# The first expert's start: two chunks of weights ahead of the gathers, another order of remainders, one comparison a round, rounded digits

## Chip, cores, metric

The kernel runs on one core of a Trainium2 chip. The metric is the device time of one execution in microseconds, as the median of several runs.

## What is computed

An attention with a causal window of 64 positions (8 batches, 8 heads, 576 positions, 64 channels) gives x, 4608 tokens of 512. A mixture of eight experts follows. Every (token, expert) pair is taken in falling order of its logit; a token goes to the first expert that still has room (576 places each). Each expert then runs its tokens through two products.

```python
logits = x @ w_gate
order = np.argsort(-logits.flatten())
for idx in order:
    tok, e = (int(idx) // E, int(idx) % E)
    if assigned[tok] >= 0 or counts[e] >= cap:
        continue
    assigned[tok] = e
    counts[e] += 1
for e in range(E):
    mask = assigned == e
    h = np.maximum(x[mask] @ w1[e], 0.0)
    out[mask] = h @ w2[e]
```

## The kernel before

Three phases lie behind one another on one core. The attention runs for about 148 us and stores x to xs in HBM. Then a routing finds, expert by expert, the threshold at which the fullest expert is filled. `Routing.steps(p)` does this for the p-th expert to be filled: for p = 0 in six rounds (`rounds`, L514) with nothing else for TensorE to do, for p = 1 to 6 in eight rounds (L657 to L780) beside the products of the expert before, for p = 7 none.

A round compares the maxima m (36 columns of 128 tokens) with 15 thresholds (`compare`, L497, in two halves of 20 and 16 columns) into G, and TensorE counts by matmuls over G (L672). When the threshold is known, the places of the taken tokens are numbered. Y (L824) holds each token's place, si its place counted from zero, sb its two digits (place div 32 and place mod 32). A (L849) marks the high digit among 18 values, B (L839) the low digit among 32. R (L851 on ScalarE, L857 on VectorE) is A times the row of the token in two parts, and 18 matmuls of R and B (L862) put the tokens' rows at their places; ils (L866), eight small matmuls (L871) and idx (L876) turn that into the list of 576 row numbers. After it, eid, un and L are brought up to date (L881 to L889) and the choices counted (L892, L896); `taken` (L899) adds the count up with one matmul (L901) and three small operations.

`Experts.turn` (L1110) gathers the rows of the list by five indirect DMAs on GpSimd's queue (L1132; four tiles of 128 rows and one of 64), transposes each tile (`across`, L1051), copies it to xh (L1122, ScalarE, rounded) and makes the remainder xl = x - xh (L1126, VectorE). `Experts.load` (L966) fetches the weights in eight chunks of 512 KB (four of w1, four of w2) into st, copies each to hi (L1017, ScalarE) and makes the remainder lo, either on VectorE (L1021, for p = 0 in the chunks 0 to 2) or by a copy on ScalarE (L1026) and an accumulating DMA on GpSimd's queue (L1028). For p = 0 the chunks 0 to 3 are fetched by SyncE's queue before the list is ready, the others by GpSimd's.

`Experts.steps` (L1271) runs the first product in units of 128 hidden columns f by 256 or 320 tokens: twelve matmuls each into one of three PSUM rooms (`room`, L957), four of hi with xh, four of lo with xh, four of hi with xl. `evac` copies the room to hh (L1280, ScalarE) and makes hl (L1285, VectorE). Two units share a chunk of w1. For p = 0 six units of the first 256 tokens come first, then six of the other 320, then the last two f. `warm` (L603) puts matmuls that feed nothing into TensorE's queue: 28 behind the list of p = 0 and six behind the first tile's transposes.

Every engine works its queue off in order. The order is fixed while the program is written: generators (`route`, `load`, `turn`, `products`) yield either an estimated time or a condition, and `Streams.run` (L1415) resumes them by a clock of its own, so that what an instruction stands behind in its queue depends on the estimates. For p = 0 `turn` puts the transposes of tile a at the moment there - 1.28 us x (4 - a), where there is 9.3 us behind the writing of the list (6.4 for the gathers, 2.9 for their landing).

Of the kernel before, what the change touches and what calls it, by code (L numbers as in the profile page):

```python
# [9 lines left out]
FT = mybir.dt.float32  # L10
# [353 lines left out]
FAR = 2.0 ** 101  # L364
OWN = 2
# [5 lines left out]
class Routing:  # L371


    def __init__(self, ctx, tc, c, V):
        self.tc, self.nc, self.c, self.V = tc, tc.nc, c, V
        nc = tc.nc
        rt = ctx.enter_context(tc.tile_pool(name="rt", bufs=1))
        self.rt, self.ctx = rt, ctx

        def t(name, shape, dt=FT):  # L380
            x = rt.tile(shape, dt, name=name)
            setattr(self, name, x)
            return x

        for name in ("eid", "un", "m", "best"):
            t(name, [128, NJ])
        for name in ("oh", "w", "one"):
            t(name, [128, NJ, E], BF)
        t("G0", [128, NJ * 64], BF)
        t("hi", [128, NJ], BF)  # L390
        t("cw", [128, E])
        t("dg", [128, 64], I32)
        t("sh", [128, NR], I32)
        t("v5", [72, 2, 4, 5], I32)
        t("lane", [128, 1])
        t("rows", [128, 1], U32)
        self.setup = self.constants(t)
        self.idx, self.eint = {}, {}

# [10 lines left out]
    def constants(self, t):  # L410
# [37 lines left out]
        for name, n, m in (("r32", 32, 2), ("r18", 18, NJ)):  # L448
            yield nc.gpsimd.iota(t(name, [128, n, m], BF), pattern=[[1, n], [0, m]], base=0, channel_multiplier=0,
                                 allow_small_or_imprecise_dtypes=True)  # L450
# [174 lines left out]
    def steps(self, p):  # L625
# [8 lines left out]
        if p < E - 1:  # L634
            if p:
                for n, f in enumerate(self.choices(0, NJ, p)):
                    f()
                    yield self.dve(490)
                    if n == 3 and p > 1:
                        yield from self.taken()  # L640

# [15 lines left out]
            for r in range(NR if p else 0):  # L657
# [4 lines left out]
                for j0, j1 in ((0, 20), (20, 36)):  # L662
                    self.compare(G, thr, j0, j1)
                    yield self.dve(420)
# [161 lines left out]
        si = tile_([128, 3, NJ], I32, name="si", bufs=1)  # L826
        nc.vector.scalar_tensor_tensor(si[:, 0], Y[:, 0], -1.0, Y[:, 1], op0=OP.add, op1=OP.add)
        yield self.dve(500)
        nc.vector.tensor_scalar(si[:, 1], si[:, 0], 5, None, op0=OP.arith_shift_right)
        nc.vector.tensor_scalar(si[:, 2], si[:, 0], 31, None, op0=OP.bitwise_and)  # L830
        sb = tile_([128, 2, NJ], BF, name="sb", bufs=1)
        nc.vector.tensor_copy(sb, si[:, 1:3])
        yield self.dve(500)
# [10 lines left out]
        Rw = R_[:, :, 0:72].rearrange("p q (k a h) -> p k a q h", k=2, h=2)  # L844

        def pairs(x):
            return x.rearrange("p a (q h) -> p a q h", h=2)

        nc.vector.tensor_tensor(A_, self.r18, sb[:, 0, None, :].to_broadcast([128, 18, NJ]), OP.is_equal)  # L849
        yield self.dve(410)  # L850
# [4 lines left out]
        for j0, j1 in ((0, NJ),) if p else ((0, 18), (18, 36)):  # L855
            n = j1 - j0
            nc.vector.tensor_tensor(Rw[:, 1, :, j0 // 2:j1 // 2], pairs(A_[:, :, j0:j1]), pairs(self.row[:, :, j0:j1].to_broadcast([128, 18, n])), OP.mult)  # L857
            if not p:
                low(j0 // 2, j1 // 2)
            yield self.dve(600) + slack + (500 if p else 0) + late  # L860
            for j in range(j0, j1, 2):
                nc.tensor.matmul(il, R_[:, j // 2], B_[:, j // 2].rearrange("p b h -> p (b h)"), start=(j == 0), stop=(j == NJ - 2))  # L862
            yield self.busy(n * 16)
# [8 lines left out]
        if p == 0:  # L872
            self.warm(28)
# [5 lines left out]
        if p < E - 1:  # L879
# [30 lines left out]
            if not p or p == E - 2:  # L910
                yield slack if p < OWN else 1500
                yield from taken()
# [22 lines left out]
class Experts:  # L935
# [30 lines left out]
    def load(self, p, ei):  # L966
# [7 lines left out]
        def fetch(i):  # L974
            st[i] = fw.tile([128, 1024], FT, name="st", bufs=STAGE)

            q, r = (nc.gpsimd, eg) if p == 0 and i >= 4 else (nc.sync, e)
# [8 lines left out]
        for i in range(ahead):  # L986
            fetch(i)
        if p == 0:
            yield lambda: self.gathered

# [12 lines left out]
        jobs = [(i, k) for i in range(2 * NCH) for k in range(2 if seven and i < NCH else 1)]  # L1003
        for i, k in jobs:
# [14 lines left out]
            yield lambda: self.gathered > p  # L1019
# [90 lines left out]
    def turn(self, p, idx):  # L1110
# [19 lines left out]
        for a in range(5):  # L1130
            n = 128 if a < 4 else 64
            nc.gpsimd.indirect_dma_start(out=g[0:n, a], out_offset=None, in_=self.xs,  # L1132
                                         in_offset=IndirectOffsetOnAxis(ap=idx[0:n, a:a + 1], axis=0))
        self.gathered += 1
# [12 lines left out]
        for tiles in ((0, 1), (2, 3), (4,)) if p else ((0,), (1,), (2,), (3,), (4,)):  # L1147
# [6 lines left out]
            if p == 0 and a < 1:  # L1154
                self.warm(6)
# [115 lines left out]
    def steps(self, p, idx):  # L1271
# [29 lines left out]
        for n, (f, c0, c1) in enumerate(units):  # L1301
            yield lambda: (p, f // 2, 0) in self.W
            yield lambda: self.tiles[p] * 128 >= c1
            wh, wl = self.W[p, f // 2, 0]
            h = self.room()[:, 0:c1 - c0]
            k = 0
            for wt, xt in ((wh, xh), (wl, xh), (wh, xl)):
# [3 lines left out]
                for cc in range(NX):  # L1311
                    nc.tensor.matmul(h, wv[:, cc, 128 * (f % 2):128 * (f % 2) + 128], xt[:, cc, c0:c1],  # L1312
                                     start=(k == 0), stop=(k == 11))
                    k += 1
                    if k % 3 == 0:
                        yield self.busy(3 * (13.5 + (c1 - c0) / 2.4))
            self.spawn(evac(f, c0, h), 100)
# [115 lines left out]
def body(tc, q, k, v, vt, wg, w1, w2, xs, out):  # L1433
    nc = tc.nc
    with ExitStack() as ctx:
# [13 lines left out]
        rt.spare = ex.room  # L1449
# [43 lines left out]
```

## Time and profile before

| | us |
|---|---|
| median of 3 runs | 643.43 |
| the runs | 643.63, 640.76, 643.43 |
| the profiled execution | 638.62 |
| its span, first to last instruction | 636.4 |
| TensorE (PE) busy | 603.9 (95%) |
| VectorE (DVE) busy | 461.6 (73%) |
| ScalarE (ACT) busy | 339.5 (53%) |
| GpSimd (POOL) busy | 217.4 (34%) |

The profile is of one execution, and its times are microseconds from its first instruction. Some 2.2 us lie outside the span. Names such as L1021 are lines of the kernel before. "out<-in" gives the tiles that an instruction writes and reads; a bracket gives the idle time of the engine just before the instruction and what ended it. PEld is the loading of weights into TensorE, SP is SyncE.

### The profile page before, as it was taken

To read this page: it belongs to the slowest core of one execution; us is meant where nothing else is said; L and a number is where in the kernel's file an instruction comes from. 1 tells how busy PE (TensorE), PEld (TensorE's weight loads), DVE (VectorE), ACT (ScalarE), POOL (GpSimd) and SP (SyncE) were. 2 spreads that over 40 slices of the span, in tenths; PEclk is the share of its full clock that TensorE was granted. 3 is DMA by queue.
4 is the path that set the end of the run, shared out by engine and by line. 5 is a ranking of instruction groups with operands and counts; after the bars stand their busy time and mean duration, and the time that the engine had idled before them with its cause. 6 is when DMAs were issued, how large, how long until landed. Compare 5 with 4: busy or idle time off the path is not lost. (4 is left out here: it accounts for less than half of the span.)

```text
span 636.4 us, 16942 instructions
## 1 busy us (share of the span) xinstructions
PE 603.9 (95%) x6395; PEld 525.3 (83%) x6395; DVE 461.6 (73%) x2043; ACT 339.5 (53%) x596; POOL 217.4 (34%) x231
## 2 busy tenths in 40 slices
PE   7899999995589999999999999999999999999995
PEld 6778888885479779988998898899789889988984
DVE  5888878887787757876786787678768776885610
ACT  2477767681255176345637446363626556666820
POOL 4355556551141061224306123331522422323211
PEclk9999999996599999999999999999999999999999
DMA  8997769993477098769679677948948556856821
GB/s 316 370 377 290 293 251 346 357 360 127 149 222 136 23 305 203 149 226 205 165 172 264 178 151 265 228 104 230 234 150 191 179 145 164 258 138 157 183 62 41
DMA packets 39760, 133.04 MB, mean 209 GB/s; under 512 B 5112, under 2 KB 5240, under 8 KB 39680
## 3 DMA queue, kind: packets, MB, share of 16 engines
q0 software_dynamic: 14992, 51.93, 36.0%
q1 hardware_dynamic: 24400, 79.52, 34.7%
q8 instruction: 50, 0.82, 0.5%
q10 hardware_dynamic: 288, 0.52, 0.3%
q14 instruction: 30, 0.25, 0.1%
HBM read 82.15 MB, written 18.87 MB: 159 GB/s over the span
## 5 line engine op out<-in xcount | busy, mean ns | idle before, releaser
L1341 POOL DMA_INDIRECT out<-ot,idx x40 | 40.6, 1016 | 196.3 <-ACT ot L1326 33.7
L1359 PE MATMUL o<-wh,hh 128*128 128x512 f32 x256 | 101.6, 397 | 0.0
L1359 PE MATMUL o<-wl,hh 128*128 128x512 f32 x256 | 101.6, 397 | 0.0
L1359 PE MATMUL o<-wh,hl 128*128 128x512 f32 x256 | 101.4, 396 | 0.0
L152 POOL TENSOR_TENSOR st<-st,mx 128x512 f32<-128x512 f32 x72 | 73.3, 1039 | 67.7 <-DVE mx L145 54.2
L1017 ACT ACTIVATE wh<-st 128x1024 fp32r<-128x1024 f32 x72 | 75.3, 1052 | 16.0 <-DVE st L999 9.0
L1280 ACT ACTIVATE hh<-h 128x256 fp32r<-128x256 f32 (+1 forms) x96 | 38.9, 407 | 71.2 <-PE h L1312 69.4
L1028 POOL DMA_DIRECT2D wl<-st x59 | 54.6, 1143 | 57.2 <-ACT wl L1026 33.0
L1132 POOL DMA_INDIRECT xg<-xs,idx x40 | 43.0, 1075 | 83.1 <-DVE eq L883 72.9
L1312 PE MATMUL h<-xh,wh 128*128 128x320 f32 (+1 forms) x384 | 70.4, 301 | 0.7 <-ACT xh L1122 0.7
L1312 PE MATMUL h<-xh,wl 128*128 128x320 f32 (+1 forms) x384 | 71.0, 300 | 0.0
L145 DVE CUSTOM_DVE_ANT_0 st<-Sp,mask 128x128 f32<-128x128 f32 x288 | 67.7, 284 | 3.1 <-PE Sp L136 2.5
L1312 PE MATMUL h<-xl,wh 128*128 128x320 f32 (+1 forms) x384 | 69.2, 298 | 0.7 <-DVE xl L1126 0.7
L1026 ACT ACTIVATE wl<-wh 128x1024 fp32r<-128x1024 f32 x59 | 62.3, 1056 | 0.8
L1312 PEld LDWEIGHTS h<-xh,wh 128*128 128x128 f32 x384 | 57.0, 189 | 1.5 <-ACT xh L1122 0.8
L1312 PEld LDWEIGHTS h<-xl,wh 128*128 128x128 f32 x384 | 56.9, 189 | 0.9 <-DVE xl L1126 0.9
L1312 PEld LDWEIGHTS h<-xh,wl 128*128 128x128 f32 x384 | 57.1, 189 | 0.2
L1359 PEld LDWEIGHTS o<-wh,hh 128*128 128x128 f32 x256 | 48.1, 188 | 9.6 <-DVE t L1213 0.6
L1359 PEld LDWEIGHTS o<-wh,hl 128*128 128x128 f32 x256 | 48.1, 188 | 9.3
L1359 PEld LDWEIGHTS o<-wl,hh 128*128 128x128 f32 x256 | 48.1, 188 | 9.0
L1326 ACT ACTIVATE ot<-o 128x512 f32<-128x512 f32 x34 | 20.2, 595 | 65.3 <-PE o L1359 61.9
L1285 DVE SCALAR_TENSOR_TENSOR hl<-h,hh 128x256 fp32r<-128x256 f32 x96 | 40.1, 418 | 14.3 <-ACT hh L1280 14.0
(276 smaller groups left out, 1256.8 us busy)
## 6 DMA issues: line engine op xcount, KB each, us to landing
st<-w SPq DMA_DIRECT2D x60, 512.0 KB, 6.6
wl<-st POOLq DMA_DIRECT2D x59, 512.0 KB, 7.0
V<-v SPq DMA_DIRECT2D x16, 584.0 KB, 8.9
xs<-x SPq DMA_DIRECT2D x36, 256.0 KB, 4.3
VT<-vt SPq DMA_DIRECT2D x8, 640.0 KB, 9.0
VT<-vt SPq DMA_DIRECT2D x8, 512.0 KB, 7.7
Q<-q SPq DMA_DIRECT2D x6, 640.0 KB, 7.0
K<-k SPq DMA_DIRECT2D x6, 640.0 KB, 8.4
```

The lines of the kernel that those rows point to most:

```text
L145: nc.vector.tensor_tensor_reduce(st[:, h, :], Sp[h % 2][:, h // 2], mk, scale=-0.125, scalar=3.0e38, op0=OP.add, op1=OP.min, accum_out=mx[ ...
L152: nc.gpsimd.tensor_tensor(st, st, mx[:, :, None].to_broadcast([128, 4, 128]), OP.subtract)
L1017: nc.scalar.activation(hi, x, AF.Copy)
L1026: nc.scalar.activation(lo, hi.bitcast(FT), AF.Copy, scale=-1.0)
L1028: nc.gpsimd.dma_start(lo.bitcast(FT), x, accum_op=OP.add)
L1132: nc.gpsimd.indirect_dma_start(out=g[0:n, a], out_offset=None, in_=self.xs, in_offset=IndirectOffsetOnAxis(ap=idx[0:n, a:a + 1], axis=0))
L1280: nc.scalar.activation(hh[:, f, c0:c1], h, AF.Relu)
L1285: nc.vector.scalar_tensor_tensor(t, h[:, a - c0:b - c0], 0.0, hh[:, f, a:b].bitcast(FT), op0=OP.max, op1=OP.subtract)
L1312: nc.tensor.matmul(h, wv[:, cc, 128 * (f % 2):128 * (f % 2) + 128], xt[:, cc, c0:c1], start=(k == 0), stop=(k == 11))
L1326: nc.scalar.activation(ot, o, AF.Copy)
L1341: nc.gpsimd.indirect_dma_start(out=self.out, out_offset=IndirectOffsetOnAxis(ap=idx[0:m, a:a + 1], axis=0), in_=ot[0:m], in_offset=None)
L1359: nc.tensor.matmul(o, ht[:, f, 128 * a:128 * a + 128], wt[:, 512 * (f % 2):512 * (f % 2) + 512], start=(f == 0 and k == 0), stop=(f == NF ...
```

## The change

For the first expert, SyncE fetches two chunks of weights, not four; chunk 2 is fetched by GpSimd between the second and the third gather, chunk 3 behind the fifth. The hi copies of chunks 0 and 1 are written together; their remainders lo wait for marks of the routing: chunk 0's until the choices of p = 0 are counted, chunk 1's until the choices of p = 1 are made and two tiles' xl are written, chunk 2's until three are. The choices of p = 1 wait before their last step for two xl. The counting up (`taken`) of p = 0 moves into the choices of p = 1. The first two units of products are interleaved: the hi and lo parts of both come before the xl parts of both. The two warm-up groups have 17 and 3 matmuls.

In each round of p = 1 to 6 one comparison covers all 36 columns. In all lists the high digit is made by adding and subtracting a constant of 1.5 x 2^28, which rounds si - 15.5 to a multiple of 32; A compares with multiples of 32, and the low digit is what is left, made behind A. R is written with the token pairs as the outer loop.

```diff
+ROUND = 1.5 * 2.0 ** 28
 (Routing.__init__)
+        self.reached = 0
 (Routing.constants)
-        for name, n, m in (("r32", 32, 2), ("r18", 18, NJ)):
-            yield nc.gpsimd.iota(t(name, [128, n, m], BF), pattern=[[1, n], [0, m]], ...
+        for name, n, m, k in (("r32", 32, 2, 1), ("r18", 18, NJ, 32)):
+            yield nc.gpsimd.iota(t(name, [128, n, m], BF), pattern=[[k, n], [0, m]], ...
 (Routing.steps, choices of p > 0)
                     f()
                     yield self.dve(490)
-                    if n == 3 and p > 1:
+                    if n == 3:
                         yield from self.taken()
+                    if n == 4:
+                        yield lambda: self.ready()
+                self.reached = 2
 (Routing.steps, rounds of p > 0)
-                for j0, j1 in ((0, 20), (20, 36)):
-                    self.compare(G, thr, j0, j1)
-                    yield self.dve(420)
+                self.compare(G, thr, 0, NJ)
+                yield self.dve(700)
 (Routing.steps, the list)
-        si = tile_([128, 3, NJ], I32, name="si", bufs=1)
-        nc.vector.scalar_tensor_tensor(si[:, 0], Y[:, 0], -1.0, Y[:, 1], op0=OP.add, op1=OP.add)
+        si = tile_([128, NJ], FT, name="si", bufs=1)
+        nc.vector.scalar_tensor_tensor(si, Y[:, 0], -16.5, Y[:, 1], op0=OP.add, op1=OP.add)
         yield self.dve(500)
-        nc.vector.tensor_scalar(si[:, 1], si[:, 0], 5, None, op0=OP.arith_shift_right)
-        nc.vector.tensor_scalar(si[:, 2], si[:, 0], 31, None, op0=OP.bitwise_and)
         sb = tile_([128, 2, NJ], BF, name="sb", bufs=1)
-        nc.vector.tensor_copy(sb, si[:, 1:3])
-        yield self.dve(500)
+        nc.vector.tensor_scalar(sb[:, 0], si, ROUND, -ROUND, op0=OP.add, op1=OP.add)
+        yield self.dve(250)
...
-        Rw = R_[:, :, 0:72].rearrange("p q (k a h) -> p k a q h", k=2, h=2)
+        Rw = R_[:, :, 0:72].rearrange("p q (k a h) -> p k q a h", k=2, h=2)
...
-            return x.rearrange("p a (q h) -> p a q h", h=2)
+            return x.rearrange("p a (q h) -> p q a h", h=2)
 
         nc.vector.tensor_tensor(A_, self.r18, sb[:, 0, None, :].to_broadcast([128, 18, NJ]), OP.is_equal)
-        yield self.dve(410)
+        nc.vector.scalar_tensor_tensor(sb[:, 1], si, 15.5, sb[:, 0], op0=OP.add, op1=OP.subtract)
+        yield self.dve(660)
...
         if p == 0:
-            self.warm(28)
+            self.warm(17)
...
             self.taken = taken
-            if not p or p == E - 2:
-                yield slack if p < OWN else 1500
+            self.reached = max(self.reached, 1)
+            if p == E - 2:
+                yield 1500
                 yield from taken()
 (Experts.load)
-            q, r = (nc.gpsimd, eg) if p == 0 and i >= 4 else (nc.sync, e)
+            q, r = (nc.gpsimd, eg) if p == 0 and i >= 2 else (nc.sync, e)
...
-        for i in range(ahead):
+        for i in range(ahead if p else 2):
             fetch(i)
         if p == 0:
+            self.amid = lambda: fetch(2)
             yield lambda: self.gathered
+            fetch(3)
...
+        if p == 0:
+            jobs = jobs[2:]
+            both = []
+            for i in range(2):
+                yield max(0, there[i] - self.clock())
+                both.append([fw.tile([128, 1024], FR, name=x, bufs=self.ring) for x in ("wh", "wl")])
+                nc.scalar.activation(both[i][0], st[i], AF.Copy)
+                yield self.busy(970, "act") + 80
+            for i, (hi, lo) in enumerate(both):
+                yield lambda: self.reached() > i and (not i or self.lows[0] > 1)
+                nc.vector.tensor_tensor(lo, st[i], hi.bitcast(FT), OP.subtract)
+                self.W[p, i, 0] = (hi, lo)
+                self.busy(1130, "dve")
+                self.taken += 1
+                fetch(i + ahead)
+                yield 100
...
-            yield lambda: self.gathered > p
+            yield lambda: self.gathered > p and (p or i > 2 or self.lows[0] > 2)
 (Experts.turn)
             nc.gpsimd.indirect_dma_start(out=g[0:n, a], ...)
+            if p == 0 and a == 1:
+                self.amid()
...
             if p == 0 and a < 1:
-                self.warm(6)
+                self.warm(3)
 (Experts.steps)
-        for n, (f, c0, c1) in enumerate(units):
-            yield lambda: (p, f // 2, 0) in self.W
-            yield lambda: self.tiles[p] * 128 >= c1
+        parts = [(n, (0, 1, 2)) for n in range(len(units))]
+        if not p:
+            parts[0:2] = (0, (0, 1)), (1, (0, 1)), (0, (2,)), (1, (2,))
+        banks = {}
+        for n, kinds in parts:
...
+            for kind in kinds:
+                wt, xt = ((wh, xh), (wl, xh), (wh, xl))[kind]
...
+            if kinds[-1] < 2:
+                continue
 (body)
-        rt.spare = ex.room
+        rt.spare, ex.reached, rt.ready = ex.room, lambda: rt.reached, lambda: ex.lows[0] > 1
```

## Rows read from the trace of the kernel before

**Rows 1.** Page, the span in 40 slices: PE's busy tenths.

```profile
PE   7899999995589999999999999999999999999995
```

**Rows 2.** Busy by stretch: stretch, PE, PEld, DVE, ACT, POOL (instructions), clock, DMA, GB/s.

```profile
160.00:180.00 20.00, 11.92 (x155) 9.28 (x155) 16.75 (x59) 6.07 (x7) 7.10 (x6) 0.68 0.45 152
```

**Rows 3.** DVE in time: start, length, engine, line, operation; digits and list.

```profile
167.24 0.20 DVE L827 SCALAR_TENSOR_TENSOR si<-Y 128x36 int32<-128x36 f32 x1
167.47 0.18 DVE L829 TENSOR_SCALAR si<-si 128x36 int32<-128x36 int32 x1
...
168.01 0.50 DVE L849 TENSOR_TENSOR A<-r,sb 128x648 bf16<-128x648 bf16 x1
...
171.22 0.17 DVE L876 CAST idx<-h 128x5 uint32<-128x5 f32 x1 [0.35 <-PE h L871]
```

**Rows 4.** PE in time (idle before, releaser in brackets): the list's matmuls.

```profile
169.46 1.14 PE L862 MATMUL rps<-B,R 128*128 128x64 bf16 x18 [2.52 <-ACT R L851]
```

**Rows 5.** POOL in time: the gathers (first three) and the fetches behind them.

```profile
171.67 1.02 POOL L1132 DMA_INDIRECT xg<-xs,idx  x1 [17.13 <-DVE eq L883]
172.99 1.79 POOL L1132 DMA_INDIRECT xg<-xs,idx  x1 [0.30 <-issue]
175.09 1.97 POOL L1132 DMA_INDIRECT xg<-xs,idx  x1 [0.31 <-issue]
...
179.91 1.70 POOL L978 DMA_DIRECT2D st<-w  x3
```

**Rows 6.** DVE in time: the first of three long remainders.

```profile
172.73 1.23 DVE L1021 TENSOR_TENSOR wl<-st,wh 128x1024 fp32r<-128x1024 f32 x1
```

**Rows 7.** PE in time: warm-up, transposes of tiles, first products.

```profile
171.08 4.46 PE L607 MATMUL rps<-r,ones 128*128 128x288 bf16 x28
...
176.01 0.51 PE L1054 MATMUL tp<-identr,xg 128*128 128x128 f32 x4 [0.26 <-DMA xg<-xs,idx]
...
177.16 0.54 PE L1054 MATMUL tp<-identr,xg 128*128 128x128 f32 x4
178.38 0.74 PE L1312 MATMUL h<-xh,wh 128*128 128x256 f32 x4 [0.69 <-ACT xh L1122]
...
180.26 0.39 PE L1312 MATMUL h<-xl,wh 128*128 128x256 f32 x1 [0.67 <-DVE xl L1126]
180.48 0.45 PE L1054 MATMUL tp<-identr,xg 128*128 128x128 f32 x4
...
181.21 0.64 PE L1312 MATMUL h<-xh,wh 128*128 128x256 f32 x4
181.68 0.41 PE L1312 MATMUL h<-xh,wl 128*128 128x256 f32 x2
```

**Rows 8.** DMA issues, us to landing: gather 2, POOL's first and last fetch.

```profile
xg<-xs,idx POOLq DMA_INDIRECT x1, 4.3
...
st<-w POOLq DMA_DIRECT2D x1, 512.0 KB, 5.1
...
st<-w POOLq DMA_DIRECT2D x1, 512.0 KB, 8.6
```

**Rows 9.** Comparisons, p = 2: DVE and PE in time; PE's waits after 185.

```profile
250.26 0.47 DVE L499 TENSOR_TENSOR G<-m,thr 128x300 bf16<-128x300 f32 x1
251.71 0.42 DVE L1285 SCALAR_TENSOR_TENSOR hl<-h,hh 128x256 fp32r<-128x256 f32 x1 [0.97 <-ACT hh L1280]
252.63 0.27 PE L672 MATMUL rps<-G 128*128 128x60 bf16 x4 [0.41 <-DVE G L499]
...
PE rps L672 <- DVE G L499: 0.7, 2, 0.4
```

**Rows 10.** Busy by stretch of 0.5 us: the clock falls and comes back.

```profile
147.50:148.00 0.50, 0.38 (x12) 0.29 (x9) 0.43 (x3) 0.50 (x1) 0.00 (x0) 1.00 0.77 287
...
149.00:149.50 0.50, 0.00 (x0) 0.00 (x0) 0.43 (x4) 0.00 (x0) 0.00 (x0) 0.50 0.01 4
...
172.50:173.00 0.50, 0.50 (x4) 0.38 (x3) 0.50 (x2) 0.50 (x1) 0.20 (x2) 0.64 1.03 410
```

More of the change, by code (lines that the diff above doesn't have):

```diff
@@ L446, in constants @@
         yield nc.vector.tensor_scalar(tab[:, 0, 7:15], tab[:, 0, 7:15], -2 ** 31, None, op0=OP.bitwise_xor)
[L448 to L449 removed]
+        for name, n, m, k in (("r32", 32, 2, 1), ("r18", 18, NJ, 32)):
+            yield nc.gpsimd.iota(t(name, [128, n, m], BF), pattern=[[k, n], [0, m]], base=0, channel_multiplier=0,
                                  allow_small_or_imprecise_dtypes=True)
@@ L856, in steps @@
             n = j1 - j0
-            nc.vector.tensor_tensor(Rw[:, 1, :, j0 // 2:j1 // 2], pairs(A_[:, :, j0:j1]), pairs(self.row[:, :, j0:j1].to_broadcast([128, 18, n])), OP.mult)
+            nc.vector.tensor_tensor(Rw[:, 1, j0 // 2:j1 // 2], pairs(A_[:, :, j0:j1]), pairs(self.row[:, :, j0:j1].to_broadcast([128, 18, n])), OP.mult)
             if not p:
@@ L1300, in steps @@
         last = [max((n for n, u in enumerate(units) if u[0] // 2 == i), default=-1) for i in range(NCH)]
-        for n, (f, c0, c1) in enumerate(units):
-            yield lambda: (p, f // 2, 0) in self.W
-            yield lambda: self.tiles[p] * 128 >= c1
+        parts = [(n, (0, 1, 2)) for n in range(len(units))]
[3 more added lines that the diff above has]
+        for n, kinds in parts:
+            f, c0, c1 = units[n]
+            if not kinds[0]:
+                yield lambda: (p, f // 2, 0) in self.W
+                yield lambda: self.tiles[p] * 128 >= c1
+                banks[n] = self.room()[:, 0:c1 - c0]
             wh, wl = self.W[p, f // 2, 0]
-            h = self.room()[:, 0:c1 - c0]
-            k = 0
-            for wt, xt in ((wh, xh), (wl, xh), (wh, xl)):
+            h = banks[n]
+            for kind in kinds:
+                wt, xt = ((wh, xh), (wl, xh), (wh, xl))[kind]
                 if xt is xl:
@@ L1311, in steps @@
                 for cc in range(NX):
+                    k = NX * kind + cc + 1
                     nc.tensor.matmul(h, wv[:, cc, 128 * (f % 2):128 * (f % 2) + 128], xt[:, cc, c0:c1],
-                                     start=(k == 0), stop=(k == 11))
-                    k += 1
+                                     start=(k == 1), stop=(k == 12))
                     if k % 3 == 0:
                         yield self.busy(3 * (13.5 + (c1 - c0) / 2.4))
+            if kinds[-1] < 2:
+                continue
             self.spawn(evac(f, c0, h), 100)
```

## The prediction

> **What bounds the kernel now.** I read the slices of the page first, then the busy times by stretch, then the order of time of each engine between 165 and 186 us. TensorE (PE) is at 9 tenths in nearly every slice, and it has one hollow, in the tenth and eleventh slice [rows 1]: the first expert's routing and the start of its products. Between 160 and 180 us it is busy for 11.92 of 20 us at a mean clock of 0.68 [rows 2]. Behind that hollow PE has no gap worth the name: the waits after 185 us name a single cause, 0.7 us in two places [rows 9]. So the kernel is bound by PE, and time can be won only where PE idles. A microsecond by which the first expert's products run earlier is a microsecond at the end, unless a new wait eats it.
>
> The chain of this start is serial. The digits of the first list are made on VectorE (DVE) from 167.24, the list is there at 171.22 + 0.17 [rows 3]; GpSimd (POOL) issues five gathers from 171.67 [rows 5]; PE transposes tile 0 at 176.01 and tile 1 at 177.16, and the first product starts at 178.38, behind the copy of tile 1 [rows 7]. Then PE waits once more: the ninth product needs the remainder xl of tile 1, until 180.26 [rows 7]. Tile 2 is transposed at 180.48, and the tenth product comes right behind (tile 2 plus about 0.3: 180.8). From there PE runs without a stop. So the figure to follow is this: **at 180.8 nine products and three transposes are done.** A product of 256 columns costs 0.12 us at full clock (four from 181.21 to 181.68) [rows 7].
>
> **The change, part by part.**
>
> **Rounded digits.** Before, four steps on 36 elements lead from Y to A: the first starts at 167.24, the second at 167.47, A at 168.01 [rows 3]. After, A needs si and one fused add; the second digit is made behind A. Two links of 0.23 replace 0.77: A starts 0.31 earlier. The second digit costs some 0.2 us, in the 0.5 us for which A runs before its readers can start. ScalarE (ACT) builds half of R from A, and PE's list waits for that until 169.46 [rows 4], so the whole 0.31 reaches the list. The new order of R's writing may make the ACT or DVE copy faster or slower; the trace has no such form. Bounds: 0.2 lost to 0.2 won, and I take 0. The list is then there 0.31 earlier (0.1 to 0.5), at 171.08, and gather 0 starts at 171.36.
>
> **Two chunks of weights instead of four ahead of the gathers.** Four chunks of 512 KB go out on SP before the list, and gather 0 shares the DMA engines with chunks 2 and 3. Gather 2, which does not, lands 4.3 us after its start, 2.3 us behind the end of its issue (175.09 + 1.97) [rows 5, 8]. Gather 0 was issued by 172.69 and used at 176.01 [rows 5, 7], 3.3 behind. After: 172.38 + 2.3, so 174.7 or 174.8 and a transpose at about 175.0.
>
> **The long remainders leave the gathers' way.** The undisturbed issue of a gather took 1.02; the second and third took 1.79 and 1.97 [rows 5]. The second ran under a remainder lo of 128x1024 on DVE (172.73, 1.23 long) and ended 0.8 behind it [rows 5, 6]; there are three such remainders before the first product. After, the first one stands behind the count of choices and p = 1's first maximum, at about 173.9. Gather 1 runs from 172.68 to 173.7 and lands at 176.0 to 176.2, against 177.1. The first product follows a transpose of tile 1 by 1.22 [rows 7]: about **177.3 instead of 178.38**.
>
> The Trainium skill, "SBUF — State Buffer", section "Who interferes with whom", says that a VectorE instruction with two SBUF inputs contends only with a GpSimd instruction that reads SBUF, and infers that descriptor generation is not held up by it. The lengths of the gathers in [rows 5] speak against that for gathers. By that rule the plain weight fetch that now follows gather 1 would take its 0.6 us whatever DVE does; held like a gather, it would put all that follows 0.8 us later.
>
> **Chunk 2 between gathers 1 and 2.** This is the new cost. POOL's queue becomes g0, g1, f2, g2, g3, g4, f3, f4. Three fetches cost 1.70, so f2 costs 0.57 [rows 5]: 173.74 to 174.3. Gather 2 starts at 174.6 under the first remainder (173.9 to 175.1) and ends 0.8 behind it, at 175.95. With nothing ahead it lands at 178.3. But 512 KB are ahead of it: the first fetch of POOL's landed 5.1 us after its start, so chunk 2 comes at 178.8, and the last of four, which had traffic around it, took 8.6 [rows 8]. Bounds for gather 2: 178.3 (the chunk does not hold it) to 181.3 (the chunk takes 6.9, midway between these two, and the gather 0.7 more). I take 179.4, nearest to the 5.1 row, since the engines are empty then, with half a chunk's time behind it.
>
> **The order of products.** Units 0 and 1 now run their first two kinds before either needs xl. By the kernel's own clock the products start 6.49 us after the list is written, tile 2's transpose stands at 7.34, and so eleven products stand ahead of it on PE, where nine did. PE could take tile 2 at 177.3 + 11 x 0.12 = 178.6; it waits until 179.5. xl of tile 1 is ready on DVE at about 178.4 and needed five products later: its wait (0.67 us) is gone, and the wait for gather 2 takes its place. After it, the twelfth product starts at 179.8. Against 180.8 with nine done that is 1.0 + 2 x 0.12 = **1.2 us won**. With the bounds of gather 2: 2.1 won to 0.7 lost.
>
> Behind that: tiles 3 and 4 land at about 180.3 and 181.2, and PE wants them at 180.9 and 181.8: free. Lo of chunk 1 is behind the two xl and p = 1's first comparison on DVE: done at 180.5, wanted at about 181.9. Chunk 2's hi waits on ACT in front of unit 0's copy, and its lo on DVE in front of unit 0's hl. With three PSUM rooms, unit 3 (183.9) needs both: 178.8, the copy of tile 2 to 180.6, 1.05 for hi, 1.23 for lo, 0.42 for hl make 183.4. Free, up to a landing at 181.2; each microsecond beyond costs one. Chunk 3, moved behind the gathers, has its products at about 202 us.
>
> **Fewer warm-up matmuls** (17 and 3 for 28 and 6) lie where PE has nothing else to do; 28 took 4.46 us [rows 7]. Priced at nothing, while the clock holds (below).
>
> **One comparison a round.** 48 pairs, of which the larger half took 0.47 [rows 9], become 48 single ones, estimated at some 0.65 (nearly twice the columns, one start instead of two). They lie beside PE's work, at no gain, but for two places: after a first half at 250.26 the second was queued behind an hl that waited 0.97 for ACT, and PE idled 0.41 [rows 9]; with the other place 0.7 in all. A single comparison can't be split so. Bounds 0 (it happens elsewhere) to 0.7; I take 0.4.
>
> **Sum:** 1.2 + 0.4 = 1.6 us. The profiled execution, 638.62 us with a span of 636.4, becomes 637.0. The median of the three runs is 643.43, 4.8 us above that execution; the same step from the median gives 641.8, and as the four executions scatter over 5 us I put the forecast at 641.5.
>
> **The rivals.** (A) **The chunk does not hold gather 2**: it lands at 178.3, PE never waits behind 177.3, and 2.1 + 0.7 + some 0.3 from a faster R make 3.1 us: 635.5 on the profiled execution, about 640 as a median. For it: the gather's data are small and sixteen engines share. Against: both stand in POOL's one queue. The Trainium skill, "DMA: Bandwidth & Descriptors", section "Anatomy of one DMA", fits a POOL transfer as about 2.0 us plus its bytes at 436 GB/s, 3.2 us for a chunk, and by that estimate this is the case that comes; the row of 5.1 [rows 8] is against it. (B) **The gain stays in the queue**: gather 2 at 180.3 or later, 0 to 0.3 us in all: 638.5, median 643. For it the 8.6 row. (C) **The clock falls, the other side.** PE ran out of the attention's matmuls before 148.0, its clock was half by 149.0, and it came back between 172.5 and 173.0, when PE had been busy with short breaks since 169.46 [rows 4, 10]. With 17 warm-ups PE stops at about 173.8 and idles to 175.0, longer than it did before that fall. If the clock halves there, each product costs 0.24 until it comes back. It decides from 1.6 us of products lost, that is from 3.2 us of work at half clock, about to 180.5; if it holds through the stretch in which 4 to 5 us are worked, 2 to 2.5 us are lost: net 0.4 to 0.9 slower, 639.3, median 644. Against it: the clock stayed full before over idle times of 0.7 between the first products [rows 7]. (D) **The edit does little**, since the first gathers land no sooner: only digits and comparisons are left, 0.7 us: 637.9, median 642.7.
>
> **How the numbers follow.** Forecast 0.5, A 0.16, B 0.12, C 0.14, D 0.08. The range takes in A with the scatter of runs (640 less 1.5) and C (644 and 0.7): 638.5 to 644.7. A measurement of this kernel can tell about 0.5% (3.2 us) from no change. Only A with the scatter on its side, and the forecast measured against a slow median, come out faster than that: 0.22; slower only C with scatter: 0.07; the rest, 0.71, within.
>
> **What would show it.** Right: gather 0's transpose near 175.0, gather 1's issue near 1.0 us, the first product near 177.3, a PE wait for gather 2 of up to 1 us, the second wait (for xl) gone, PE at full clock from 173 on, no wait of PE for the comparison. Wrong: a clock of 0.5 between 174 and 181 (C), unit 3 waiting for its room (a late chunk 2), gather 0 still some 3 us behind its issue (D), or PE waits past 182 us.

## The result, and the profile after

The changed kernel is slower: 645.25 us as the median of 14 runs, against 642.16 for the kernel before on the same chip. The ratio is 1.0054, with a 95% interval of 1.0034 to 1.0073, so by the ratio some 3.5 us were lost (3.1 between the medians) where 1.6 to be won were forecast. The forecast was 641.5 with a range of 638.5 to 644.7. The profiled execution took 646.55 us with a span of 644.9.

The first expert's start came out nearly as forecast. In this execution all that lies ahead of Y (attention and rounds) took 2.68 us longer. DVE in order of time, Y of before and Y of after:

```profile
166.97 0.23 DVE L824 SCALAR_TENSOR_TENSOR Y<-h,X 128x72 f32<-128x72 f32 x1 [0.31 <-PE h L821]
169.65 0.23 DVE L829 SCALAR_TENSOR_TENSOR Y<-h,X 128x72 f32<-128x72 f32 x1 [0.31 <-PE h L826]
```

With these 2.68 us taken off, the rows of after compare directly with those of before. First POOL of after, in order of time (start, length, engine, line, operation, idle before), the answer to [rows 5].

```profile
174.20 1.02 POOL L1155 DMA_INDIRECT xg<-xs,idx  x1 [16.99 <-DVE eq L887]
175.52 1.05 POOL L1155 DMA_INDIRECT xg<-xs,idx  x1 [0.30 <-issue]
176.58 0.61 POOL L983 DMA_DIRECT2D st<-w  x1
177.50 1.31 POOL L1155 DMA_INDIRECT xg<-xs,idx  x1 [0.30 <-issue]
```

DVE of after, in order of time, the answer to [rows 3, 6].

```profile
170.36 0.49 DVE L852 TENSOR_TENSOR A<-r,sb 128x648 bf16<-128x648 bf16 x1
...
176.72 1.23 DVE L1021 TENSOR_TENSOR wl<-st,wh 128x1024 fp32r<-128x1024 f32 x1
```

PE of after, in order of time, the answer to [rows 4, 7].

```profile
171.84 1.29 PE L866 MATMUL rps<-B,R 128*128 128x64 bf16 x18 [2.23 <-ACT R L855]
...
177.61 0.75 PE L1077 MATMUL tp<-identr,xg 128*128 128x128 f32 x4
...
180.32 0.74 PE L1345 MATMUL h<-xh,wh 128*128 128x256 f32 x4 [0.69 <-issue]
...
181.73 0.46 PE L1077 MATMUL tp<-identr,xg 128*128 128x128 f32 x4
```

Tile 0 is transposed at 174.93 (177.61 less 2.68), the second gather's issue takes 1.05 instead of 1.79, the first product stands at 177.64 instead of 178.38, eleven products are done ahead of tile 2 instead of nine, and no product waits for xl. Up to the start of the first expert's last matmul PE needed 74.66 us from Y in the kernel before and 72.41 in this one: 2.25 us less. Not all of that is won. Eight transposes of the second expert's rows now stand behind the first expert's last product instead of ahead of it. PE in order of time, two rows of before and two of after:

```profile
240.69 0.80 PE L1054 MATMUL tp<-identr,xg 128*128 128x128 f32 x8
241.86 0.52 PE L1312 MATMUL h<-xh,wh 128*128 128x256 f32 x3
242.29 0.52 PE L1345 MATMUL h<-xh,wh 128*128 128x256 f32 x3
242.64 0.80 PE L1077 MATMUL tp<-identr,xg 128*128 128x128 f32 x8
```

They take 0.63 us, from 242.64 to the next product, so some 1.6 us are won.

The loss comes at the second expert. These are PE's waits between 186 and 640 us (in all, times, longest), to be held against the one row of before in [rows 9].

```profile
PE h L1345 <- DVE st L689: 1.9, 1, 1.9
PE rps L677 <- DVE G L502: 1.5, 1, 1.5
PE h L1199 <- DMA wl<-st: 1.1, 1, 1.1
PE o L1393 <- ACT ot L1360: 0.5, 1, 0.5
```

The first two waits stand together. PE of after, in order of time (idle before and its releaser in brackets):

```profile
255.99 0.71 PE L1345 MATMUL h<-xh,wh 128*128 128x256 f32 x4 [1.94 <-DVE st L689]
...
258.47 0.63 PE L677 MATMUL rps<-G 128*128 128x60 bf16 x9 [1.53 <-DVE G L502]
...
260.35 1.27 PE L1345 MATMUL h<-xh,wh 128*128 128x320 f32 x4
```

ACT of after, in order of time, over the same stretch:

```profile
253.88 1.06 ACT L1040 ACTIVATE wh<-st 128x1024 fp32r<-128x1024 f32 x1 [4.09 <-DMA st<-w]
254.84 0.42 ACT L1305 ACTIVATE hh<-h 128x320 fp32r<-128x320 f32 x1
```

The releaser that the wait of 1.94 names is a small DVE operation. The cause is on ACT, as the experiments below show: at 249.8 it comes to hi of chunk 6 and waits 4.09 us for that chunk to land, and behind it stands the copy of the fourth product unit (254.84), which frees a PSUM room. There are three rooms; PE fills the other two and stops at the seventh unit. DVE's hl of that unit waits for the same copy, and a round's small steps and its comparison stand behind it in DVE's queue, which makes the second wait. Then the clock falls. Stretches of after: us, PE, PEld, DVE, ACT, POOL, clock, DMA, GB/s:

```profile
256.00:257.00 1.00, 0.94 (x6) 0.73 (x6) 0.86 (x6) 1.00 (x3) 1.00 (x2) 1.00 0.00 0
257.00:258.00 1.00, 0.00 (x0) 0.00 (x0) 0.97 (x5) 0.97 (x2) 1.00 (x3) 0.58 0.64 262
258.00:260.00 2.00, 1.53 (x14) 1.53 (x15) 1.42 (x6) 0.89 (x2) 2.00 (x3) 0.50 1.00 197
260.00:262.00 2.00, 2.00 (x10) 2.00 (x10) 1.26 (x7) 0.38 (x1) 0.28 (x1) 0.50 1.10 209
262.00:264.00 2.00, 2.00 (x10) 2.00 (x10) 1.09 (x3) 0.21 (x1) 0.00 (x0) 0.50 1.05 207
264.00:266.00 2.00, 2.00 (x24) 1.96 (x24) 0.76 (x3) 0.61 (x2) 0.00 (x0) 1.00 1.05 207
```

For over 6 us products run at the lower level, 1.2 GHz: four of 320 columns take 1.27 us where others take 0.75. Summed over stretches of 1 us (PE's busy time times what the clock lacks) that is 2.75 us.

The same place in the kernel before, ACT in order of time, shows that the weakness was there already, at a small price:

```profile
250.29 1.06 ACT L1017 ACTIVATE wh<-st 128x1024 fp32r<-128x1024 f32 x1 [1.61 <-DMA st<-w]
251.26 0.42 ACT L1280 ACTIVATE hh<-h 128x320 fp32r<-128x320 f32 x1
```

Why is chunk 6 no earlier, when PE is? There are six buffers for landing weights, so SP's fetch of chunk 6 waits until the addition of chunk 0's remainder (a DMA issued on POOL behind the second expert's gathers) has read its buffer. POOL of before in order of time, and SP's fetches of chunks 6 and 7:

```profile
228.56 1.01 POOL L1132 DMA_INDIRECT xg<-xs,idx  x1 [3.90 <-DVE eq L883]
...
234.94 1.03 POOL L1028 DMA_DIRECT2D wl<-st  x1
236.27 1.03 POOL L1341 DMA_INDIRECT out<-ot,idx  x1 [0.30 <-ACT wh L1017]
...
239.93 3.91 SPq L978 DMA_DIRECT2D st<-w  x2
```

The same of after:

```profile
230.44 1.01 POOL L1155 DMA_INDIRECT xg<-xs,idx  x1 [4.75 <-DVE eq L887]
...
237.38 1.01 POOL L1375 DMA_INDIRECT out<-ot,idx  x1 [0.30 <-PE o L1393]
238.38 3.79 POOL L1051 DMA_DIRECT2D wl<-st  x4
...
243.20 2.89 SPq L983 DMA_DIRECT2D st<-w  x2
```

From Y, the second expert's gathers start at 60.79 instead of 61.59: only 0.8 us earlier, since its list hangs on DVE's rounds and not on PE's products. And the planner, whose clock has PE earlier, now issues a scatter of the first expert's output ahead of the first addition. Fetch 6 goes out 73.55 us behind Y instead of 72.96, while PE starts the second expert's products 72.64 us behind Y instead of 74.89.

The account of the two profiled executions, from Y to the last matmul (462.36 and 468.03): first expert -2.25; second +5.87, of which 2.73 are more waits (3.47 against 0.74), 2.75 the clock, and the rest the transposes put off, by and large; third to fifth +0.62; last three +1.43 (the waits for wl and ot above).

### The profile page after: what moved, and what is told of

Same layout as the page of the kernel before. It is cut to its first block, busy times and chain, and to the rows that moved or that the text cites. A ratio compares the mean times of both kernels' runs of the same rounds, so it can differ in the third digit from the quotient of the medians.

```text
span 644.9 us, 16849 instructions
## 1 busy us (share of the span) xinstructions
PE 607.1 (94%) x6381; PEld 527.4 (82%) x6381; DVE 457.2 (71%) x1987; ACT 340.2 (53%) x596; POOL 218.1 (34%) x233
## 5 line engine op out<-in xcount | busy, mean ns | idle before, releaser
L1040 ACT ACTIVATE wh<-st 128x1024 fp32r<-128x1024 f32 x70 | 73.4, 1052 | 12.5 <-DMA st<-w 8.1
L1345 PE MATMUL h<-xh,wh 128*128 128x320 f32 (+1 forms) x384 | 72.7, 305 | 2.6 <-DVE st L689 1.9
L1155 POOL DMA_INDIRECT xg<-xs,idx x40 | 41.5, 1036 | 75.3 <-DVE eq L887 65.0
```

The source lines that it names most:

```text
L1040: nc.scalar.activation(hi, x, AF.Copy)
```

## Experiments

**The comparison, undone and alone.**

```diff
 (in the changed kernel; the reverse in the kernel before)
-                self.compare(G, thr, 0, NJ)
-                yield self.dve(700)
+                for j0, j1 in ((0, 20), (20, 36)):
+                    self.compare(G, thr, j0, j1)
+                    yield self.dve(420)
```

> The changed kernel with one part undone: a round's comparison is again made in two halves (columns 0 to 20 and 20 to 36). Everything at the first expert stays changed. Theory (second expert's weights): in the profiled execution of the changed kernel PE loses time at the start of the second expert, where it waits 1.94 and 1.53 us and then runs at half clock for some 6 us, because a copy of weights (hi of chunk 6) waits on ACT for its landing, ahead of a copy that frees a PSUM room. The comparison has no part in that, so this kernel takes what the changed one takes, 645 (643.5 to 646.5), 0.3 to 0.7 slower if one comparison has its own gain, and the wait of PE at the seventh unit of the second expert is there again. Rival (the comparison): the longer comparison, 0.72 us that cannot be split, holds DVE and the waits behind it are the loss; then this kernel comes back to the kernel before less the gain of the first expert's start, 640 to 641.5, and the wait is gone.

> The kernel before with one part of the change alone: one comparison a round. Theory (second expert's weights): no loss, within 1 us of the kernel before (641 to 643), the two waits of PE for a second half (0.41 and 0.33) gone. Rival (the comparison): 2 to 4 us slower than the kernel before, with waits of PE behind DVE in the rounds of the second and later experts.

Measured: the changed kernel with two halves 1.0042 (1.0020 to 1.0064); the kernel before with one comparison 1.0024 (0.9998 to 1.0049). So one comparison alone doesn't make the change slow. But the first run was not the copy of the changed kernel that was expected, and what it loses is in part another loss. Its PE waits from 186 us on:

```profile
PE h L1200 <- ACT xh L1094: 1.7, 1, 1.7
PE rps L678 <- DVE G L502: 1.1, 1, 1.1
PE h L1200 <- ACT xh L1106: 0.4, 1, 0.4
PE h L1346 <- DMA wl<-st: 0.3, 1, 0.3
```

The wait of 1.94 us at the seventh unit, which was expected again, is gone: the stall at the second expert shrank to 1.14, ACT's wait for chunk 6 to 2.11, and the clock held there. Here the first expert took 1.4 us longer: the clock fell to half again from 177.7 to 181.1, in the first products. That is rival C of the prediction, in one of seven profiled executions with the thinner warm-up. PE came later by this, but the second expert's gathers started 1.8 us later too. So the smaller stall isn't explained by the late PE, and a share of the comparison in its size isn't ruled out. Instead 1.7 us came up at the seventh expert's start, where the planner had put its work in another order. In the run of one comparison alone the two waits of 0.41 and 0.33 were gone, with no idle time of PE from 235 to 300 us. But there chunk 6 held nothing up in the first place. ACT of that run, in order of time, hi of chunk 6 with no wait for its landing:

```profile
250.72 1.05 ACT L1016 ACTIVATE wh<-st 128x1024 fp32r<-128x1024 f32 x1
```

The second expert's gathers started 1.04 us earlier from Y than in the kernel before, and PE's first product of that expert 1.45 later. So this run doesn't show that the comparison removed the waits. It lost 2.44 us much later, at 551, on a landing (wl), and the clock was at half for 3.4 us behind that.

**Room first: two of the second expert's copies ahead of chunk 6.** Only ACT's order changes.

```diff
+            late = self.late.append if (p, i) == (1, 6) else lambda f: f()
-            nc.scalar.activation(hi, x, AF.Copy)
+            late(lambda hi=hi, x=x: nc.scalar.activation(hi, x, AF.Copy))
 (likewise lo and its addition; in evac, behind the copy into hh)
+            self.copied += p == 1
+            while self.copied > 4 and self.late:
+                self.late.pop(0)()
```

> The changed kernel with four ACT instructions and one of POOL in another order and nothing else: at the second expert hi and lo of chunk 6 are issued behind the copies of the fourth and fifth product unit instead of ahead of them, so that a PSUM room comes free without waiting for that chunk. Theory (second expert's weights): the waits of 1.94 and 1.53 us at its start fall to under 0.5 together, the clock stays full behind them, and the kernel takes 5 to 6 us less in that stretch than the changed kernel's profiled execution and keeps the earlier start: 640 to 641.5 as a median, 1 to 2 below the kernel before. Rival (the loss is elsewhere: the comparison, the thinner warm-up, or the later experts' order): 645, like the changed kernel, whether these waits go or not. Second rival: the stall only moves to a later unit (chunk 6's own landing or hl on DVE) and 643 to 644 are left.

**First addition first: one exchange on POOL.**

```diff
+            if (p, a) == (0, 1):
+                self.late.append(send)      (the scatter, issued behind the first addition of p == 1)
+            else:
+                send()
```

> The changed kernel with two POOL instructions exchanged and nothing else: behind the second expert's gathers the first addition of remainders (of its chunk 0) is issued before the third scatter of the first expert's output, as in the kernel before. The buffer of chunk 0 comes free about 1 us earlier, and so the fetch of chunk 6 starts and lands about 1 us earlier. Theory (second expert's weights): the first wait of 1.94 us falls to about 1, the two together from 3.5 to about 2 to 2.5; if the clock still falls the kernel gains 1 us over the changed one (644), if it then holds 3 to 4 us (641.5 to 642.5). Rival (this order is the whole cause): the waits are gone and 640 to 641.5 come. Rival (the loss is elsewhere): 645.

Measured: room first 1.0018 (0.9994 to 1.0041), first addition first 1.0002 (0.9972 to 1.0033). The changed kernel stands at 1.0054, so the first cure takes some 2.3 us off and the exchange of two DMA issues some 3.3. These are estimates: each ratio is to the kernel before in the same series of runs, and the changed kernel was measured in the first series alone. In neither profile does the clock fall behind the stall. PE's waits of the run with room first, from 186 us on, the two at the second expert:

```profile
PE h L1350 <- DVE dg L683: 1.5, 1, 1.5
PE rps L677 <- DVE G L502: 1.2, 1, 1.2
```

And all of those of the run with the first addition first:

```profile
PE rps L677 <- DVE G L502: 1.8, 2, 1.4
```

Room first went as its second rival said: the stall moved on. The copies of chunks 6 and 7 now stood as a block of four, 4.2 us on ACT, ahead of the sixth unit's. First addition first brought hi of chunk 6 2.25 us forward (81.98 us behind Y instead of 84.23), more than the 1 us expected. 1.8 us of waits were left.

**Both cures, in both kernels.** hi and lo of chunks 6 and 7 are now issued one by one behind the copies of the fifth to eighth unit; the changed kernel also gets the exchange on POOL.

```diff
+            late = self.late.append if p == 1 and i > 5 else lambda f: f()
 (in evac, behind the copy into hh: hi, then lo and its addition, in turns)
+            self.copied += p == 1
+            for _ in range(2 - self.copied % 2 if p == 1 and self.copied > 4 else 0):
+                if self.late:
+                    self.late.pop(0)()
```

> The kernel before with ACT's order changed at the second expert and nothing else: hi and lo of chunks 6 and 7 are issued one by one behind the copies of the fifth to eighth product unit, instead of ahead of the fourth to sixth. Theory (second expert's weights): the kernel before has this weakness too, but reaches the place 2.25 us later; its two waits of PE there (0.41 and 0.33) go and it gains 0.5 to 1 us: 0.998 to 0.999 of the kernel before. Rival (the order costs nothing there): no change, and the waits stay. Should it gain 2 or more, then the stall also comes in most executions of the kernel before and not just in those of the changed one.

> The changed kernel with both cures at the second expert: the first addition of remainders ahead of the third scatter on POOL, and hi and lo of chunks 6 and 7 spread one by one behind the copies of the fifth to eighth product unit on ACT. Theory (second expert's weights): with either cure alone 1.8 and 2.8 us of waits were left there, because the four copies of the two chunks still stood in one block ahead of the sixth unit's; spread, under 0.4 is left, and the earlier start of the first expert (2.25 us in the profiled execution) comes through to the end: 1 to 2 us below the kernel before, ratio 0.997 to 0.9985. Rival (the gain is lost elsewhere): ratio 1.000 or above although the waits are gone; then the later stretches of the trace, or the clock at the first expert's start, show where it went.

Measured: the kernel before with the spread copies 0.9983 (0.9969 to 0.9996), the changed kernel with both cures 0.9969 (0.9955 to 0.9984), 636.73 us against 639.29. Neither profile has a wait of PE at the second expert; in that of the cured kernel PE waits nowhere between 186 us and the end. Its ACT at the place, with no wait for a landing:

```profile
249.34 0.44 ACT L1310 ACTIVATE hh<-h 128x320 fp32r<-128x320 f32 x1 [1.67 <-PE h L1354]
249.83 1.06 ACT L1043 ACTIVATE wh<-st 128x1024 fp32r<-128x1024 f32 x1
```

From Y to the last matmul the cured kernel takes 459.80 us, the kernel before with the spread copies 461.58 and the kernel before 462.36. This version beats both kernels. The two cures are worth some 5.4 us by the ratios (1.0054 to 0.9969); in the traces the second expert takes 58.87 us instead of 65.42, and most of the rest is waits of the last three experts. The change itself, measured against a kernel before that has its cure too, is worth 1.8 us in the traces, 1.3 between the medians (638.04 and 636.73) and 0.0014 (0.9 us) between the ratios, whose intervals overlap.

**The warm-up**, 28 and 6 in place of 17 and 3, in the cured and in the changed kernel.

```diff
-            self.warm(17)
+            self.warm(28)
-                self.warm(3)
+                self.warm(6)
```

> The kernel with both cures, and with the 28 and 6 warm-up matmuls of the kernel before in place of 17 and 3; nothing else. In four profiled executions with 17 and 3 the clock came back at 173.8, 174.8 and 178.7, and in one it fell to half again from 177 to 181. Theory (thin warm-up): with 28 and 6 the clock is back by 175.5 and stays; as a median 0.5 to 1.5 us less than with 17 and 3, even though a few warm-ups may delay the first transposition by up to 0.5. Rival (the warm-up is nothing): the same time within 0.5 us, or 0.5 us slower where PE is still warming up when the first tile lands.

> The changed kernel with 28 and 6 warm-up matmuls instead of 17 and 3, nothing else. Theory (second expert's weights as the main loss): the waits of 1.5 to 3.5 us and the block on ACT at the second expert's start are there again, and the kernel is 1.5 to 3 us slower than the kernel before. Rival (the thin warm-up is the main loss): it comes back to 0.5 to 1.5 below the kernel before.

Measured: 0.9979 (0.9967 to 0.9991) for the cured kernel, where 17 and 3 gave 0.9969: no gain. The changed kernel stays slow, 1.0068 (1.0052 to 1.0084, six runs), and shows the stall a second time, in nearly the same figures:

```profile
PE rps L677 <- DVE G L502: 2.5, 2, 1.5
PE h L1345 <- DVE st L689: 1.9, 1, 1.9
PE h L1199 <- DMA wl<-st: 0.3, 1, 0.3
```

Of the 2.5 us, 1.54 lie there and 1.00 at the third expert, at 317 us. The clock is at 0.5 again from 254.8 to 261.6 us, at a cost of 2.89 us.

**The waits filled with work.** 28 matmuls whose results nobody uses, right ahead of the two waits of the changed kernel.

```diff
+                if p == 1 and n == 6:
+                    spare = self.ps.tile([128, NX, 128], FR, name="tp", bufs=2) ...
+                    for _ in range(14):
+                        nc.tensor.matmul(spare[:, 0:256], self.W[p, 0, 0][0][:, 0:128], xh[:, 0, 0:256], ...)
 (and 14 more behind the sixth product of that unit)
```

> The changed kernel with 28 matmuls of 256 columns added on PE at the second expert, 14 right ahead of the wait of 1.94 us and 14 right ahead of the wait of 1.53; their results are used by nothing. At 0.11 to 0.12 us each they take some 1.6 us a place, inside the waits as the profiles of the changed kernel show them. Theory (the clock makes the stall dearer): PE is not idle, so the granted clock stays at 1.0 behind the stall where it was 0.5 for 6 to 7 us in two profiled executions, and the 2.75 to 2.9 us that this cost are saved: ratio to the kernel before 1.000 to 1.003. Rival (the clock falls for another reason, or not in most executions): no gain, 1.004 to 1.007.

Measured: 1.0018 (0.9999 to 1.0036), against 1.0054. ACT waits 4.07 us for chunk 6 as before, PE does nothing more of use than it did, and yet about 2.3 us come back by the ratios, whose intervals just overlap; in the traces the second expert takes 62.73 us instead of 65.42. The stretches of this run, columns as above:

```profile
254.00:256.00 2.00, 1.75 (x15) 1.57 (x15) 1.36 (x7) 2.00 (x5) 1.23 (x2) 1.00 0.01 2
256.00:257.00 1.00, 1.00 (x11) 1.00 (x10) 0.93 (x6) 0.97 (x2) 1.00 (x3) 1.00 0.64 262
257.00:258.00 1.00, 1.00 (x17) 0.94 (x16) 0.63 (x1) 1.00 (x2) 1.00 (x2) 1.00 0.76 148
258.00:260.00 2.00, 2.00 (x20) 2.00 (x16) 1.76 (x8) 0.49 (x2) 1.51 (x2) 1.00 1.06 201
```

The clock holds, and the 2.69 us are what it cost before (2.75). So in these two executions the half clock is the doing of PE's idle time, and about half of the stall's price.

**The other order without the early PE**: the kernel before, with the third scatter ahead of the first addition.

```diff
+                if (p, i) == (1, 0):
+                    self.behind.append(add)      (issued behind the third scatter)
+                else:
+                    add()
```

> The kernel before with two POOL instructions exchanged and nothing else: behind the second expert's gathers the third scatter of the first expert's output is issued ahead of the first addition of remainders, as in the changed kernel. PE reaches the second expert as late as before. Theory (it takes both, the early PE and the late chunk): chunk 6 lands about 1 us later, the waits of PE there grow from 0.74 to 1.5 to 2 us, the clock holds in most executions: 0.8 to 1.5 us slower, ratio 1.001 to 1.0025. Rival (the order alone is the cause): the whole loss of the changed kernel, ratio 1.004 to 1.006. Rival (the early PE alone): no change, under 1.001.

Measured: 1.0026 (1.0009 to 1.0044). One wait of 1.60 us stands at the second expert instead of 0.74 in all, and the clock holds. From the first expert's last matmul to the second's the traces have 59.55 us in the kernel before, 60.14 here (the late chunk alone), 61.00 with the first addition first (the early PE alone) and 65.42 in the changed kernel (both). So neither makes the loss alone. The ratio holds more than these 0.6 us: the seventh expert took 2.1 us longer here, 1.3 of them waits near 553 us, which this theory doesn't cover.

**The comparison in two halves, in the cured kernel.** Edit as in the first experiment.

> The kernel with both cures, and a round's comparison again in two halves. Theory (the price of the comparison as predicted, 0.4 us with bounds 0 and 0.7): 0 to 0.7 us more than with one comparison, ratio 0.997 to 0.9985 to the kernel before, with waits of PE for a second half back in the second expert. Rival (one comparison has no part in the gain): 0.9965 to 0.997, no waits. Rival (one comparison costs, as its run alone, 1.0024 with an interval from 0.9998, hints): under 0.996.

Measured: 1.0009 (0.9984 to 1.0034), above every figure of the theories. No wait for a second half came back. What came is the wait that the first experiment had shown, 1.71 us for ACT at the seventh expert's start, with the clock at half behind it, from 530 to 534 us:

```profile
PE h L1205 <- ACT xh L1099: 1.7, 1, 1.7
```

The seventh expert takes 54.57 us instead of 50.27, of which the wait is 1.71 and the clock 1.68. Beside the early start, then, one comparison is worth more than 0.4 in these runs, for a reason that I had not considered: with one piece in place of two, and an estimate of 700 in place of twice 420, the planner puts the queues of POOL, ACT and DVE in another order up to the seventh expert. Which of these differences makes the wait was not tested.

The gap at the second expert orders most of these runs. The gap is the start of chunk 6's hi on ACT less PE's first product of that expert; beside it PE's waits there:

| kernel | gap, us | PE's waits, us |
|---|---|---|
| before, one comparison | 6.19 | 0 |
| before | 8.43 | 0.74 |
| changed, first addition first | 9.31 | 1.82 |
| before, scatter first | 9.63 | 1.60 |
| changed, two halves | 11.07 | 1.14 |
| changed, 28 and 6 warm-ups | 11.56 | 3.45 |
| changed, waits filled | 11.58 | filled |
| changed | 11.59 | 3.47 |

Either a chunk that is later or a PE that is earlier widens it. (In the changed kernels 0.63 us of it goes to the transposes put off.) With two halves, DVE's queue differs, and less is lost at the same gap.

## Why the prediction was wrong

**The step that failed** is in its first paragraph: "Behind that hollow PE has no gap worth the name", and from it "A microsecond by which the first expert's products run earlier is a microsecond at the end, unless a new wait eats it." That PE doesn't wait says how things stand at the old time; it says nothing of the margin. The second expert's weights ran on a clock of their own (list, gathers, additions, free buffers, fetch 6, ACT), 0.8 us earlier, and PE came 2.25 earlier. The prediction searched for the new wait only up to unit 3 of the first expert. So the chunk's lateness stood in the sum at nothing; it cost 3.47 us of waits and 2.75 of clock. Of the prediction's own signs of being wrong two came: a clock of 0.5 between 174 and 181, which isn't the loss (see the rivals), and PE waits past 182 us, which are.

**The sign stood in its own rows.** In [rows 9] hl waits 0.97 us for ACT's hh, and PE 0.41 for the comparison behind it. I read this as the price of a comparison that is split in two. ACT's queue at that time shows hi of chunk 6 with a wait of 1.61 for its landing: a stall that had just begun to reach PE. The kernel before with the spread copies still compares in two halves, and it has neither wait. So the 0.4 us that the sum gave to one comparison was the chunk's price, and the run of one comparison alone, where hi of chunk 6 waited for nothing, doesn't speak against that.

**The first expert's start, step by step.** Digits: PE's list begins 0.30 earlier, forecast 0.31; but its 18 matmuls took 1.29 us instead of 1.14 [rows 4], and gather 0 starts only 0.15 earlier. Tile 0: 174.93, forecast 175.0. The second gather's issue: 1.05, forecast 1.02. First product: 177.64, forecast 177.3. xl: no wait, right. Gather 2: here rival A was right. In the cured kernel it starts 0.92 us behind gather 1's issue and lands 4.1 us after its start, with 4.3 for the chunk ahead of it; [rows 8] had 4.3 for a gather with nothing ahead. I had taken 4.8. PE comes to tile 2 with eleven products done and waits for nothing, so the first expert was over 2.25 us sooner, some 1.6 of it won, where I had 1.2 with a bound of 2.1. For the chunk, the Trainium skill's fit ("DMA: Bandwidth & Descriptors", section "Anatomy of one DMA") gives 3.2 us, an estimate; the measured 4.3 lies between it and the 5.1 that I took from [rows 8], and rival A, the case that it spoke for, came.

The fetch between the gathers ran beside a remainder on DVE from 176.72 and took 0.61 us; the gather behind it took 1.31 and ended 0.86 behind the remainder's end. The rule of the Trainium skill ("SBUF — State Buffer", section "Who interferes with whom"), that descriptor generation isn't held up, is an inference there; the fetch agrees with it, and the gather does not. The gather also reads its row numbers (idx) from SBUF, so the other half of the rule, that such an instruction does contend, may be what holds it; no run here tells these apart.

**The rivals.** A was right in its mechanism and wrong in its end. B and D did not come. C came, a little: in the changed kernel the clock was back only at 178.7, ahead of the first product (at 172.4 to 175.4 in the other six with 17 and 3, at 172.9 and 174.4 with 28 and 6), and it fell again in one other execution, at a cost of about 1.4 us; 28 warm-ups brought no gain in either kernel, so it isn't the loss. The rival on the other side that came true, a stall at the second expert, was not among them. The range, 638.5 to 644.7, was the scatter around a gain; it left out any loss that starts behind 186 us.

**What stays open.** Waits of 0.3 to 2.4 us in the last three experts (on wl, ot and xh) come and go between executions whose orders there are the same: the changed kernel had 1.1 for wl, and 0.3 with 28 warm-ups. In the profile of one comparison alone such a wait (2.44 us, and 1.67 of clock behind it) outweighs what was gained at the second expert; there the queues of the last experts are ordered otherwise than in the kernel before, so this may be order or chance. No run tells how much of the scatter of 5 us is theirs. Rounded digits and R's new order were not run alone.

## What to carry to other kernels

Before a stage that PE waits on is made faster, look at the next stages for the resources that don't move with it, and write down by how much each is ahead; a releasing engine that itself waits for a landing, as ACT with 1.61 us here, is a stage with no margin even where PE shows no gap. In an engine's queue, nothing that waits for a transfer should stand ahead of the copy that frees a PSUM room. A planner that orders by its own clock reorders distant queues when one estimate changes, so compare the orders of all queues before and after, DMA issues first.

## What the runs showed of the hardware that I had not expected

A short stall of TensorE can cost more than its length. With two waits of 1.9 and 1.5 us, and 0.95 us of matmuls between them, the granted clock fell to 0.5 in the second and stayed there for 6.8 us, in both profiled executions of that order (2.75 and 2.89 us lost); with 1.5 and 1.2, with 1.4 and 0.4, and with a single 1.6 it stayed at 1.0; after one of 1.7 at 530 us it fell in one execution and not in another, after one of 2.4 at 549 us it fell. With matmuls of no use in the waits it stayed at 1.0, which gave back some 2.3 us of the 3.5 by the ratios, 2.69 in the traces.
